# Attention with an MLP behind it: q's scale factor moves into GpSimd's cast, k and q are cast ahead of v, and four loads move behind a DMA transpose

## Chip, cores, metric

One core of a Trainium2 chip runs the whole program. The metric is the device time of one execution in microseconds. Engines are named as the profile names them: PE (TensorE), PEld (its weight loads), DVE (VectorE), ACT (ScalarE), POOL (GpSimd), SP (SyncE, which here only issues DMAs).

## The reference

Attention over 8 batches of 12 heads with 448 positions of 64 numbers, with a softmax that has one more term in its denominator, then an MLP with a Mish-like gate over the 3584 tokens. q, k, v, the weights and the output are f32.

```python
def _attn_ref(q, k, v):                      # each (8, 12, 448, 64)
    scale = 1.0 / np.sqrt(q.shape[-1])       # 1/8
    scores = scale * np.matmul(q, k.transpose(0, 1, 3, 2))
    m = np.max(scores, axis=-1, keepdims=True)
    e = np.exp(scores - m)
    attn = e / (np.sum(e, axis=-1, keepdims=True) + np.exp(-m) + 1e-09)
    return np.matmul(attn, v)

def _moe_ref(x, w_in, w_out):                # x (3584, 768), w_in (768, 2048), w_out (2048, 768)
    h = x @ w_in
    sp = np.where(h > 20.0, h, np.log1p(np.exp(np.minimum(h, 20.0))))
    return (h * np.tanh(sp)) @ w_out
```

## The kernel before

**Pairs and units.** Two heads of a batch are a pair; there are 48 pairs, 6 to a batch. Three pairs are a unit (`UNIT_PAIRS`), so a batch is two units and pair p belongs to unit p // 3. The first six pairs run in a loop of their own (the head). The main loop then runs over units `u`, with `p0 = 3u` the unit's first pair and `nxt = p0 + 3` the next unit's first pair. A unit has 12 steps `n` (four a pair) of attention, mixed with pieces of the second MLP product (L567), and then eight blocks `f` of the first MLP product (L514) of a batch whose attention is done. Attention ends with unit 15; what follows is MLP alone.

**A pair's way.** SP loads q, k and v of a pair (`load_pair`, L135), each as 112 rows of 512 f32 numbers, into buffers of which there are three for each of q, k and v. `cast` turns them to bf16 on POOL (L186); from pair 1 on all casts are POOL's. q and k must then be turned so that the head's 64 numbers lie along the partitions. Up to pair 17 PE does this and DVE copies the result out with the factor 1/8. From pair 18 on (`BY_DMA_FROM`), `turn_by_dma` (L197) has two DMA transposes do it, one for the three k of a unit and one for its three q; then `evac_qk` writes each pair's q into the block-diagonal tile `qd` (two halves of 64 partitions, one for each head), with the factor 1/8, as two POOL instructions (L268). The scores (L327) are PE's; DVE takes the negative maximum (L348), ACT the exponentials (L361) into `en`. At the end of a unit's steps DVE divides (`normalise`, L430), and a DMA transpose on SP turns `en` into `eT` (L438). In the next unit PE multiplies `eT` by v (`av_pair`, L478): the products of pairs p0-3, p0-2 and p0-1 stand in PE's order just ahead of the fourth score step of pairs p0, p0+1 and p0+2, and the scores run three steps ahead of the exponentials, so they come at about n = 0, 4 and 8.

**When things are issued.** Each engine and SP's queue work in the order written here. In units 2 to 4 loads and casts are spread over steps 0, 3 and 6. From unit 5 on, step 0 does it all for a unit: POOL copies two numbers out of the unit before's last `en` into `marks` (L714), which holds POOL back until that is divided; then the casts and the transposes; then some loads:

```python
for p_ in range(p0 - UNIT_PAIRS + 1, p0 + 1):      # the v casts
    if "v" in loaded.get(p_, ()):
        cast(p_, "v")
for i in range(UNIT_PAIRS):                        # the k and q casts of the next unit
    cast(nxt + i, "kq")
turn_by_dma(nxt)
load_pair(nxt + UNIT_PAIRS, "kq")
for i in range(UNIT_PAIRS):
    load_pair(p0 + 1 + i, "v")
```

So v is loaded for pairs p0+1 to p0+3 and cast in the next unit: unit 6 (p0 = 18) casts v of 16, 17, 18. In unit 5 only v of pair 15 is left to cast. In units 5 to 14 there are k and q to cast; unit 15 casts v only.

The k and q of the two remaining pairs of the unit after next are loaded at step 11 (`n == steps - 1`), from unit 4 on (`u >= first_mm2`, where `first_mm2` is 4). In unit 4 these are pairs 19 and 20. The first blocks of the first MLP product follow: at f = 0 the unit's first pair is divided and its transpose issued (pair 12 in unit 4), at f = 3 and f = 7 the other two (13 and 14), which are divided there.

Weights of the second MLP product are still being loaded through POOL's queue (L169) during unit 4.

Of the kernel before, what the change touches and what calls it, by code (L numbers as in the profile page):

```python
# [12 lines left out]
ALU = mybir.AluOpType  # L13
AX = mybir.AxisListType

UNIT_PAIRS = 3
# [3 lines left out]
def kernel(  # L20
# [9 lines left out]
    nc = tc.nc  # L30

    B, H, S, D = q.shape
# [14 lines left out]
    SCALE = 1.0 / float(D) ** 0.5  # L47
# [55 lines left out]
    QB = S // 64  # L103
# [68 lines left out]
    def cast(p, names):  # L172
        if p >= N_PAIRS:
            return
        by_t = "p h (t d) -> p t h d"
        to = casted.setdefault(p, {})
        for nm in names:
            src = loaded[p].pop(nm)
            if nm != "v":
                to[nm] = (q_cast if nm == "q" else k_cast)[:, p % UNIT_PAIRS]  # L180
            else:
                to[nm] = bf_pool.tile([SP_, 2, NT * D], BF16, tag="v_bf", name="v_bf", bufs=7)
            if nm != "v":
                src = src.rearrange(by_t, t=NT)
            if p > 0 or nm == "v":
                nc.gpsimd.tensor_copy(out=to[nm], in_=src)  # L186
                continue
            cuts = (0, NT) if nm == "k" else (0, NT // 2, NT)
            for lo, hi in zip(cuts, cuts[1:]):
                nc.vector.tensor_copy(out=to[nm][:, lo:hi], in_=src[:, lo:hi])  # L190
# [42 lines left out]
    def evac_qk(p, act=False):  # L233
        if p >= N_PAIRS:
            return
        by_dma = p >= BY_DMA_FROM
        by = nc.gpsimd if by_dma else nc.vector
        kT = kT_all[:, p % (2 * UNIT_PAIRS)]
        (q_ps, k_ps), own = ((qT_all[:, p % UNIT_PAIRS], kT), []) if by_dma else qkT[p]
        mo_free.extend(own)  # L240
        q_reads = []
        qd = q_diag[p % len(q_diag)]
        if p < DIAG_FROM:
            qT = qd.rearrange("d i h r -> d (i h r)")[:, 0:S]
            qkT[p] = (qT, kT)
            if p == 0:
                nc.scalar.copy(kT, k_ps[:, 0:S])
                by_2 = sc_tiles[2][:, 0, :].bitcast(BF16)
                for ps, half in (q_ps, slice(0, S // 2)), (by_2, slice(S // 2, S)):
                    nc.vector.tensor_scalar(  # L250
                        out=qT[:, half], in0=ps[:, half], scalar1=SCALE, scalar2=None,
                        op0=ALU.mult,
                    )
                return
            if act:
                nc.scalar.mul(qT, q_ps[:, 0:S], SCALE)
            else:
                q_reads.append(nc.vector.tensor_scalar(
                    out=qT, in0=q_ps[:, 0:S], scalar1=SCALE, scalar2=None, op0=ALU.mult
                ))  # L260
        else:
            qkT[p] = (qd, kT)
            if p < DIAG_FROM + len(q_diag):
                nc.vector.memset(qd[0:64, :, 1, :], 0.0)
                nc.vector.memset(qd[64:128, :, 0, :], 0.0)
            for h in range(2):
                rows = slice(64 * h, 64 * h + 64)
                q_reads.append(by.tensor_scalar(  # L268
                    out=qd[rows, :, h, :],
                    in0=q_ps[rows, 0:S].rearrange("d (i r) -> d i r", i=QB),  # L270
                    scalar1=SCALE, scalar2=None, op0=ALU.mult,
                ))
        if by_dma:
            return
        if own and not act:
            nc.vector.tensor_copy(out=kT, in_=k_ps[:, 0:S])
        else:
            k_read = nc.scalar.copy(kT, k_ps[:, 0:S])
            if not own:
                apart(k_read, *q_reads)  # L280
# [298 lines left out]
    steps = UNIT_PAIRS * STEPS  # L579
# [90 lines left out]
    for u in range(UNITS_PER_B, N_UNITS + 2 * UNITS_PER_B):  # L670
# [11 lines left out]
        for n in range(steps):  # L682
            pi, s = divmod(n, STEPS)
            p, idx = p0 + pi, p0 * STEPS + n
            late_tp = u == UNITS_PER_B and n == STEPS
            exps(idx)
            if u == UNITS_PER_B + 1 and n == 0:
                for j in range(2):
                    turn_on_pe(HEAD, j, busy_first=3)
            flush_late()  # L690
            if late_tp:
                transpose_pair(p0 + 2)
                evac_qk(p0 + 2)
            if held and n == 1:
                late.extend(held)
                held.clear()
                flush_late()
            late.extend(slow)
            slow.clear()
            acc += weight[n]  # L700
            want = int(total * acc / sum(weight) + 1e-6)
            while done < want:
                fn, w = filler.popleft()
                fn()
                done += w
            scores_ahead(end)
            if n in LOAD_AT and u <= first_mm2:
                at = p0 + LOAD_AT.index(n)
                load_pair(at + LEAD, "qk")
                load_pair(at + 1, "v")  # L710
                cast(at + LEAD - 1, "qk")
                cast(at, "v")
            elif n == 0 and u <= N_UNITS:
                nc.gpsimd.tensor_copy(  # L714
                    out=marks[0:1, 3, 0:2], in_=att[p0 - 1]["en"][0:1, NT - 1, NTILE - 1, 0:2]
                )
                for p_ in range(p0 - UNIT_PAIRS + 1, p0 + 1):
                    if "v" in loaded.get(p_, ()):
                        cast(p_, "v")
                for i in range(UNIT_PAIRS):  # L720
                    cast(nxt + i, "kq")
                turn_by_dma(nxt)
                load_pair(nxt + UNIT_PAIRS, "kq")
                for i in range(UNIT_PAIRS):
                    load_pair(p0 + 1 + i, "v")
            if s == 0 and u > first_mm2:
                evac_qk(nxt + pi)
            if n == steps - 1 and u >= first_mm2:
                for i in range(1, UNIT_PAIRS):
                    load_pair(nxt + UNIT_PAIRS + i, "kq")  # L730
            for pe, n0 in BY_PE.items():
                j = n - n0
                first = 2 if pe == HEAD else 0
                if pe // UNIT_PAIRS == u - 1 < first_mm2 - 1 and first <= j < NT:
                    turn_on_pe(pe, j, busy_first=1)
            spread = RDEN_AT.get(u - UNITS_PER_B, {})
            if n in spread:
                on_act = u < first_mm2
                spread_rden(
                    spread[n], copy=nc.scalar.copy if on_act else nc.vector.tensor_copy,  # L740
                    behind=slow if on_act else late,
                )
            early = AV_AT.get(u - UNITS_PER_B)
            if early is not None and n == 7:
                keep_busy(6, bank=mo_free[0])
            if early is not None:
                if n in early:
                    av_pair(early[n], half=p)
            elif s == (2 if pi else 0) and N_PAIRS <= p < N_PAIRS + UNIT_PAIRS:
                av_pair(p - UNIT_PAIRS)  # L750
            if u - UNITS_PER_B < len(W_AT):
                at = (u - UNITS_PER_B, n)
                load_w(W_AT[at[0]].get(n, 0), behind=W_BEHIND.get(at))
# [5 lines left out]
        for f in range(FF_U):  # L759
            if moe:  # L760
                mm1_mish(b, w * FF_U + f)
            if u == UNITS_PER_B and f == 3:
                load_w(3, behind=p0 + 2)
            if not attn:
                continue
            if f == 0:
                denominators(p0, UNIT_PAIRS)
                for p in todo if p0 < LATE_DIV else todo[:1]:
                    normalise(p, dma=p not in BY_PE)
            if f == 5 and u == UNITS_PER_B + 1:  # L770
                spread_rden(p0, copy=nc.scalar.copy)
            if f == 4:
                scores_ahead(min(nxt * STEPS + 1, N_PAIRS * STEPS))
            if f in (1, 3, 5):
                if nxt < BY_DMA_FROM:
                    transpose_pair(nxt + f // 2, bank=f // 2 % 2)
                    evac_qk(nxt + f // 2)
            if f >= FF_U - 2:
                scores_ahead(min(nxt * STEPS + f - FF_U + 4, N_PAIRS * STEPS))
            if f in (3, FF_U - 1) and p0 >= LATE_DIV:  # L780
                p = todo[1 + f // (FF_U - 1)]
                normalise(p, dma=p not in BY_PE)
# [32 lines left out]
```

## Time and profile before

| | us |
|---|---|
| median of 3 runs | 471.48 (470.95 to 472.93) |
| the profiled execution, its own time | 475.91 |
| its span, first to last instruction | 474.1 |
| mean granted clock of TensorE in it | 0.993 |

| engine | busy us | instructions |
|---|---|---|
| PE | 449.2 | 3051 |
| DVE | 347.5 | 657 |
| ACT | 331.6 | 877 |
| POOL | 180.8 | 258 |

How to read the rows that follow. A group's row has line, engine, operation, what it writes and reads, partitions x elements with types, how often; then busy us, mean ns of one, idle us of the engine just before them and what ended that. A timeline's row has start (us from the span's start), length in us, engine, line and operation; rows of like instructions on end are merged (x3), and a bracket gives the idle time ahead of it. "SPq" is SP's queue: an issued DMA, whose length is the time of issuing it. A row of a stage's busy times has the window, its length, then busy us (and count) of PE, PEld, DVE, ACT and POOL, the granted clock, the DMA engines' share and GB/s.

### The profile page before, as it was taken

The numbers are of one execution on the slowest core, as the hardware profiler recorded it, in microseconds if no ns is written. First come the engines' busy times: TensorE is split into PE (matmuls) and PEld (weight loads), VectorE is DVE, ScalarE is ACT, GpSimd is POOL, SyncE is SP. The second block draws the span as 40 slices with busy tenths as digits, with TensorE's granted clock in tenths as the row PEclk, the third lists the DMA queues.
The fourth block names the chain that finished last, engine by engine and source line by source line (L and its number), as shares of the span: only waits on it lengthen the run. The fifth ranks groups of instructions, "written<-read, shape, count | busy, mean of one in ns | idle before, by whom it ended". The sixth has DMA issues, their size and how long they took to land.

```text
span 474.1 us, 8841 instructions
## 1 busy us (share of the span) xinstructions
PE 449.2 (95%) x3051; PEld 245.8 (52%) x3051; DVE 347.5 (73%) x657; ACT 331.6 (70%) x877; POOL 180.8 (38%) x258
## 2 busy tenths in 40 slices
PE   7778888999889999999999999999999999999996
PEld 3344445555535555555555555555555555556563
DVE  5999738759859798989898888989798979421021
ACT  5998848879747887978686869687887869211300
POOL 4613609105126455455463644646464620100000
PEclk9999999999989999999999999999999999999999
DMA  8999999999999999999999999999999594921122
GB/s 253 228 115 244 220 216 209 174 214 252 185 239 280 222 273 231 261 250 230 259 233 287 212 224 242 282 233 268 217 273 235 155 213 128 225 76 33 35 57 77
DMA packets 232493, 97.94 MB, mean 207 GB/s; under 512 B 189312, under 2 KB 228992, under 8 KB 232448
## 3 DMA queue, kind: packets, MB, share of 16 engines
q1 hardware_dynamic: 224928, 91.06, 84.9%
q0 software_dynamic: 7488, 6.29, 9.2%
q8 instruction: 24, 0.39, 0.4%
q14 instruction: 21, 0.17, 0.1%
q10 hardware_dynamic: 32, 0.02, 0.0%
HBM read 45.61 MB, written 11.01 MB: 119 GB/s over the span
## 4 chain that ended last, share of the span: by engine, by line
PE 68%; ACT 6%; DVE 5%; DMA 3%; issue 1%; SPq 0%; DVEq 0%; ACTq 0%
PE mo L514 24%; PE mo L567 24%; PE sc L327 8%; PE sc L478 6%; ACT en L361 6%; DVE negm L348 4%; PE sc L514 4%; DMA eT<-en 3%; PE mo L478 1%; DVE xT L491 1%; PE mo L288 0%; DMA out_dram<-o_sb 0%; DVE o_sb L550 0%; PE sc L220 0%; DVE eT L453 0%
## 5 line engine op out<-in xcount | busy, mean ns | idle before, releaser
L361 ACT ACTIVATE en<-sc,negm 128x448 bf16<-128x448 f32 x336 | 208.8, 643 | 27.3 <-DVE negm L348 25.5
L348 DVE TENSOR_REDUCE negm<-sc 128x2 f32<-128x896 f32 x192 | 182.6, 970 | 50.2 <-PE sc L327 39.6
L567 PE MATMUL mo<-w_out_sb,gT 128*128 128x384 bf16 (+1 forms) x1024 | 167.4, 307 | 0.4 <-DVE rb L418 0.4
L514 PE MATMUL mo<-xT,w_in_sb 128*128 128x448 bf16 x672 | 139.0, 352 | 2.8 <-DMA w_in_sb<-in_moe_w_in_dram 2.6
L567 PEld LDWEIGHTS <-gT 128*128 128x128 bf16 x1024 | 96.6, 98 | 56.6 <-issue 2.9
L520 ACT ACTIVATE gT<-mo 128x448 bf16<-128x448 f32 x112 | 59.4, 543 | 82.2 <-PE mo L514 81.8
L514 PEld LDWEIGHTS <-w_in_sb 128*128 128x128 bf16 x768 | 74.0, 98 | 72.0 <-DMA w_in_sb<-in_moe_w_in_dram 3.8
L268 POOL TENSOR_SCALAR qd<-qT_all 64x448 bf16<-64x448 bf16 x60 | 80.1, 1335 | 61.7 <-DMA qT_all<-q_cast 32.6
L430 DVE TENSOR_SCALAR en<-en,rden 128x448 bf16<-128x448 bf16 x252 | 85.5, 413 | 0.5
L361 ACT ACTIVATION_READ_ACCUMULATOR en<-sc,negm 128x1 f32 x336 | 72.2, 215 | 0.0
L327 PE MATMUL sc<-kT_all,qd 128*128 128x448 bf16 x252 | 72.2, 356 | 0.0
L550 DVE COPY o_sb<-mo 128x384 f32<-128x384 f32 (+1 forms) x64 | 31.9, 498 | 48.3 <-PE mo L567 48.1
L478 PE MATMUL sc<-eT,v_bf 112*64 112x448 bf16 x336 | 40.2, 360 | 5.4 <-DMA eT<-en 3.6
L186 POOL CAST q_cast<-q_f 112x512 bf16<-112x512 f32 x47 | 28.6, 608 | 32.6 <-PE mo L409 18.6
L327 PEld LDWEIGHTS <-qd 128*128 128x128 bf16 x252 | 24.7, 98 | 29.2 <-issue 13.4
L714 POOL COPY marks<-en 1x2 bf16<-1x2 bf16 x12 | 2.1, 175 | 96.3 <-DVE en L430 96.3
L478 PEld LDWEIGHTS <-v_bf 112*64 112x64 bf16 x384 | 20.0, 109 | 24.1 <-issue 7.4
L186 POOL CAST k_cast<-k_f 112x512 bf16<-112x512 f32 x47 | 28.5, 607 | 0.6 <-DMA k_f<-in_k_dram 0.3
L186 POOL CAST v_bf<-v_f 112x512 bf16<-112x512 f32 x48 | 28.1, 605 | 1.5 <-DMA v_f<-in_v_dram 1.1
L514 PE MATMUL sc<-xT,w_in_sb 128*128 128x448 bf16 x96 | 20.8, 352 | 0.0
L491 DVE CAST xT<-sc 128x448 bf16<-128x448 f32 x33 | 20.3, 615 | 0.0
L520 ACT ACT_TABLE_LOAD x14 | 18.0, 1283 | 0.8 <-PE mo L514 0.3
(63 smaller groups left out, 245.2 us busy)
## 6 DMA issues: line engine op xcount, KB each, us to landing
k_f<-in_k_dram SPq DMA_DIRECT2D x48, 224.0 KB, 5.0
q_f<-in_q_dram SPq DMA_DIRECT2D x48, 224.0 KB, 4.8
v_f<-in_v_dram SPq DMA_DIRECT2D x48, 224.0 KB, 5.1
w_in_sb<-in_moe_w_in_dram POOLq DMA_DIRECT2D x12, 256.0 KB, 10.7
w_out_sb<-in_moe_w_out_dram POOLq DMA_DIRECT2D x8, 384.0 KB, 13.3
out_dram<-o_sb SPq DMA_DIRECT2D x7, 336.0 KB, 4.1
out_dram<-o_sb SPq DMA_DIRECT2D x8, 288.0 KB, 5.1
out_dram<-o_sb SPq DMA_DIRECT2D x8, 240.0 KB, 3.7
```

Source lines behind the costliest of these rows:

```text
L186: nc.gpsimd.tensor_copy(out=to[nm], in_=src)
L268: q_reads.append(by.tensor_scalar(out=qd[rows, :, h, :], in0=q_ps[rows, 0:S].rearrange("d (i r) -> d i r", i=QB), scalar1=SCALE, scalar2=N ...
L327: nc.tensor.matmul(sc[:, bk, 0:S], lhsT=qT[:, i].rearrange("d h r -> d (h r)"), rhs=kT, start=True, stop=True,)
L348: half_max[p] = nc.vector.tensor_reduce(out=negm, in_=sc[:, 0 : len(cols), 0:S], axis=AX.X, op=ALU.max, negate=True)
L361: e = nc.scalar.activation(out=st["en"][:, :, c, 0:SP_], in_=sc[:, bk, 0:S].rearrange("q (j c) -> q j c", j=NT), func=AF.Exp, bias=st["neg ...
L430: nc.vector.tensor_scalar(out=en[:, :, i, 0:SP_], in0=en[:, :, i, 0:SP_], scalar1=st["rden"][:, i : i + 1], scalar2=None, op0=ALU.mult,)
L478: mm = nc.tensor.matmul(av[h * 64 : (h + 1) * 64, 0:S], lhsT=v_bf[:, h, j * D : (j + 1) * D], rhs=e_h, start=(j == 0), stop=(j == NT - 1),)
L491: read = nc.vector.tensor_copy(out=to, in_=av[:, 0:S])
L514: nc.tensor.matmul(h_ps[:, 0:S], lhsT=w_in_sb[:, dm, ff * 128 : (ff + 1) * 128], rhs=xT[b][:, dm, :], start=(dm == 0), stop=(dm == DM_T - 1),)
L520: nc.scalar.activation(out=gT[:, ff, b % 2 * S : b % 2 * S + S], in_=h_ps[:, 0:S], func=AF.Mish)
L550: nc.vector.tensor_copy(out=o_sb[:, cols.start : cols.start + n_dve], in_=st["o"][:, 0:n_dve])
L567: nc.tensor.matmul(st["o"][:, 0:n_cols], lhsT=gT[:, ff, i * 128 : (i + 1) * 128], rhs=w_out_sb[:, ff, cols], start=(ff == 0), stop=(ff == ...
```

## The change

Three edits, and the factor 1/8 is applied once in either version:

- For pairs from 18 on, q's cast on POOL (112x512, f32 to bf16) becomes a multiplication by 1/8 of the same tile (30 instructions in units 5 to 14). The 60 POOL multiplications that wrote `qd` become plain copies of the same 64x448 bf16 numbers.
- At step 0 of units from 5 on, the k and q casts stand ahead of the v casts in POOL's order. In SP's order nothing moves by this.
- In unit 4, the loads of q and k of pairs 19 and 20 are issued after the transpose of pair 12 instead of at step 11 ahead of it. On SP they now stand between the transposes of pairs 12 and 13. Later units keep their place.

```diff
@@ cast
+            if nm == "q" and p >= BY_DMA_FROM:
+                nc.gpsimd.tensor_scalar(
+                    out=to[nm], in0=src, scalar1=SCALE, scalar2=None, op0=ALU.mult
+                )
+                continue
             if p > 0 or nm == "v":
                 nc.gpsimd.tensor_copy(out=to[nm], in_=src)
                 continue
@@ evac_qk
-        by = nc.gpsimd if by_dma else nc.vector
...
-                q_reads.append(by.tensor_scalar(
-                    out=qd[rows, :, h, :],
-                    in0=q_ps[rows, 0:S].rearrange("d (i r) -> d i r", i=QB),
-                    scalar1=SCALE, scalar2=None, op0=ALU.mult,
+                q_h = q_ps[rows, 0:S].rearrange("d (i r) -> d i r", i=QB)
+                if by_dma:
+                    nc.gpsimd.tensor_copy(out=qd[rows, :, h, :], in_=q_h)
+                    continue
+                q_reads.append(nc.vector.tensor_scalar(
+                    out=qd[rows, :, h, :], in0=q_h, scalar1=SCALE, scalar2=None, op0=ALU.mult,
                 ))
@@ the main loop, step 0
+                for i in range(UNIT_PAIRS):
+                    cast(nxt + i, "kq")
                 for p_ in range(p0 - UNIT_PAIRS + 1, p0 + 1):
                     if "v" in loaded.get(p_, ()):
                         cast(p_, "v")
-                for i in range(UNIT_PAIRS):
-                    cast(nxt + i, "kq")
                 turn_by_dma(nxt)
@@ the main loop, step 11
-            if n == steps - 1 and u >= first_mm2:
+            if n == steps - 1 and u > first_mm2:
                 for i in range(1, UNIT_PAIRS):
                     load_pair(nxt + UNIT_PAIRS + i, "kq")
@@ the main loop, first MLP product, f == 0
                 for p in todo if p0 < LATE_DIV else todo[:1]:
                     normalise(p, dma=p not in BY_PE)
+                if u == first_mm2:
+                    for i in range(1, UNIT_PAIRS):
+                        load_pair(nxt + UNIT_PAIRS + i, "kq")
```

## The prediction

> **What bounds the kernel now.** I read the page first: engines, the chain of waits, the costliest groups.
>
> ```profile
> span 474.1 us, 8841 instructions
> ...
> PE 449.2 (95%) x3051; PEld 245.8 (52%) x3051; DVE 347.5 (73%) x657; ACT 331.6 (70%) x877; POOL 180.8 (38%) x258
> ...
> PE 68%; ACT 6%; DVE 5%; DMA 3%; issue 1%; SPq 0%; DVEq 0%; ACTq 0%
> ...
> L268 POOL TENSOR_SCALAR qd<-qT_all 64x448 bf16<-64x448 bf16 x60 | 80.1, 1335 | 61.7 <-DMA qT_all<-q_cast 32.6 <-PE sc L327 13.5 <-PE sc L478 12.0
> ```
>
> PE sets the end; POOL, which most of the change touches, is busy for 38%. An average over stages hides what matters, so I cut the steady part into units (a unit is three pairs, some 25.3 us) and asked for each stage's busy times:
>
> ```profile
> 159.60:185.30 25.70, 25.27 (x168) 14.45 (x169) 22.88 (x43) 20.22 (x55) 13.24 (x17) 1.00 1.13 244
> 185.30:210.60 25.30, 25.30 (x152) 13.20 (x153) 22.63 (x42) 20.20 (x54) 13.12 (x17) 1.00 1.06 261
> ...
> 337.20:362.50 25.30, 25.30 (x152) 13.20 (x153) 21.91 (x42) 20.25 (x54) 13.12 (x17) 1.00 0.99 247
> ```
>
> The first numbers are the window, its length and PE's busy time: 25.27 of 25.70, then 25.30 of 25.30. PE has no slack in a steady unit. Making POOL cheaper there brings nothing, and any wait that PE is given is paid in full. The one DMA wait of the chain lies earlier. In order of time the chain shows it, and PE's timeline shows the gap:
>
> ```profile
> 118.32 14.29 DMA eT<-en
> ```
>
> ```profile
> 132.66 1.38 PE L478 MATMUL sc<-eT,v_bf 112*64 112x448 bf16 x8 [3.58 <-DMA eT<-en]
> 139.19 0.95 PE L478 MATMUL sc<-eT,v_bf 112*64 112x448 bf16 x8
> 144.12 0.95 PE L478 MATMUL sc<-eT,v_bf 112*64 112x448 bf16 x8
> ```
>
> PE stands still for 3.58 us, from 129.08, until the turning of pair 12 lands at 132.6. These three rows are the value products (L478) of pairs 12, 13 and 14.
>
> **Part one: the four loads.** SP's timeline before that wait:
>
> ```profile
> 111.45 0.31 SPq L135 DMA_DIRECT2D k_f<-in_k_dram  x1
> 111.82 0.45 SPq L135 DMA_DIRECT2D q_f<-in_q_dram  x1
> 114.65 0.31 SPq L135 DMA_DIRECT2D k_f<-in_k_dram  x1
> 115.02 0.45 SPq L135 DMA_DIRECT2D q_f<-in_q_dram  x1
> 118.32 19.90 SPq L438 DMA_TRANSPOSE eT<-en  x3
> ```
>
> The first four rows are the loads of pairs 19 and 20, issued before the three turnings of unit 4. The transfers run without a gap, and their rate stands last here:
>
> ```profile
> 111.45:118.30 6.85, 6.85 (x55) 4.17 (x55) 6.07 (x16) 6.51 (x18) 5.14 (x8) 1.00 1.11 270
> ```
>
> Four loads of 224 KB are 0.92 MB, and 0.92 MB at 270 GB/s is 3.4 us of transfers that no longer lie ahead of pair 12's turning. It lands at about 132.66 - 3.4 = 129.3, against 129.08 when PE wants it: 0.2 us of wait is left. The wait had a second price, read from the granted clock (the last number but two):
>
> ```profile
> 129.62:133.03 3.41, 0.38 (x4) 0.25 (x6) 0.00 (x0) 1.49 (x6) 3.20 (x6) 1.00 1.25 233
> 133.04:136.44 3.40, 3.40 (x14) 1.32 (x11) 1.16 (x2) 0.72 (x2) 0.00 (x0) 0.50 1.30 219
> ```
>
> PE was busy for 0.38 of 3.41 us, and the next 3.40 us ran at half the clock. From pair 12's product to pair 13's are 6.53 us here (139.19 - 132.66), from pair 13's to pair 14's 4.93: the half clock cost 1.6. Stall and clock together are 3.58 + 1.6 = 5.2 us.
>
> Not all of that is won, because the loads now stand ahead of pair 13's turning, the next thing in SP's queue:
>
> ```profile
> L438 SPq DMA_TRANSPOSE eT<-en x1: 3738/3738/3738, 130.5 to 130.5; - x1
> ...
> DMA to landing us min/median/max: 6.8/6.8/6.8
> ```
>
> It was issued at 130.5 and landed 6.8 later, at 137.3. Now its issue follows pair 12's 3.4 us earlier but four load issues later (0.8 us a pair by the rows above, so 1.6): at 128.7, landing at 135.5 if the loads ahead of it cost nothing, at 138.9 if they cost all their 3.4. I take the middle, 137.2. PE wants it at 139.19 - 5.2 + 0.2 = 134.2, so 3.0 us of wait come back. Part one gains 5.2 - 0.2 - 3.0 = 2.0 us, bounds 0 (all comes back) and 5.2. In POOL's queue the casts of pairs 19 and 20 now wait for these loads, and v's cast behind them. The cover is wide: pair 18's diagonal copies run from 143.57, its first score (the x2 row) follows at 151.69, and both are shifted alike.
>
> ```profile
> 143.57 6.96 POOL L268 TENSOR_SCALAR qd<-qT_all 64x448 bf16<-64x448 bf16 x5 [10.76 <-DMA qT_all<-q_cast]
> ```
>
> ```profile
> 151.69 0.54 PE L327 MATMUL sc<-kT_all,qd 128*128 128x448 bf16 x2
> ```
>
> **Part two: the order and price of the casts.** Each unit from 6 on starts with a mark on POOL, three v casts, then six casts of k and q. Of the v casts the first one is wanted soonest: v is loaded one unit ahead for pairs p0+1 to p0+3, so unit 6 casts v of 16, 17, 18, and its PE stream multiplies by v of 15, 16, 17. Hence the second value product of a unit (pair 16) waits for the first v cast of that same unit. POOL, then PE:
>
> ```profile
> 159.31 0.17 POOL L714 COPY marks<-en 1x2 bf16<-1x2 bf16 x1 [7.37 <-DVE en L430]
> 159.43 1.72 POOL L186 CAST v_bf<-v_f 112x512 bf16<-112x512 f32 x3
> 161.10 0.60 POOL L186 CAST k_cast<-k_f 112x512 bf16<-112x512 f32 x1
> 161.66 0.60 POOL L186 CAST q_cast<-q_f 112x512 bf16<-112x512 f32 x1
> ...
> 163.89 0.60 POOL L186 CAST q_cast<-q_f 112x512 bf16<-112x512 f32 x1
> ```
>
> ```profile
> 159.57 0.95 PE L478 MATMUL sc<-eT,v_bf 112*64 112x448 bf16 x8
> ...
> 164.50 0.95 PE L478 MATMUL sc<-eT,v_bf 112*64 112x448 bf16 x8
> ```
>
> Before, that cast was done 0.72 us after the mark, and PE came for it 164.50 - 159.31 = 5.19 us after. In the last unit that the change touches the distance is the same, 5.20:
>
> ```profile
> 362.20 0.17 POOL L714 COPY marks<-en 1x2 bf16<-1x2 bf16 x1 [7.27 <-DVE en L430]
> ```
>
> ```profile
> 367.40 0.95 PE L478 MATMUL sc<-eT,v_bf 112*64 112x448 bf16 x8
> ```
>
> From 159.31 to 362.20 are eight periods, so nine units, 6 to 14 (unit 5 casts only v of 15, wanted in unit 6; unit 15 casts no k or q).
>
> Now the first v cast comes behind three k casts and three q operations that are no longer casts but multiplications. A cast's pitch is 0.56 us (161.10 to 161.66). What a GpSimd multiplication of 112x512 f32 costs no row shows, so it is bounded from both sides:
>
> ```profile
> L268 POOL TENSOR_SCALAR qd<-qT_all x60: 1321/1334/1522, 143.6 to 378.7; 64x448 bf16<-64x448 bf16 x60
> ```
>
> ```profile
> L714 POOL COPY marks<-en 1x2 bf16<-1x2 bf16 x12 | 2.1, 175 | 96.3 <-DVE en L430 96.3
> ```
>
> Below stands the cast of the same tile, 0.60 us. Above stands the multiplication of 448 elements, 1335 ns, scaled to 512: 1.53, or with a fixed 0.175 (the two-element copy) 0.175 + 1.16 x 512/448 = 1.50. It is the same operation on the same engine, only its source is f32 and its shape differs; per element it takes 2.98 ns where the cast takes 1.18. I take 1.50. Then the first v cast ends 0.12 + 3 x 0.56 + 3 x 1.50 + 0.60 = 6.9 us after the mark, where PE comes at 5.2: a wait of 1.7 us. Behind it in PE's queue stand the pair's last score and the out-projection, and DVE's maximum and ACT's exponentials wait for that score. As PE has no slack and the next mark follows PE through DVE's L430, each unit pays anew: 9 x 1.7 = 15.3 us. PE first waits when a q operation costs more than (5.2 - 0.12 - 1.68 - 0.60) / 3 = 0.93 us.
>
> The Trainium skill speaks against this price: "GPSIMD Engine Reference", section 4.1, calls one-input elementwise work on GpSimd roughly line-rate. By that q's factor would cost what its cast does, and the sum would hold only part one's gain; this trace has 2.98 ns an element against it for a one-input multiplication.
>
> The rest is hidden. The plain diagonal copies should cost near the cast's 0.53 us for 448 instead of 1335 ns (bounds 0.5 and 1.34): no matter, since nothing waits for L268 beyond the 8 us cover shown for pair 18. The turnings of k and q wait for casts that end at 6.3 after the mark instead of 5.2, when SP is still issuing k's turning. The v loads on SP wait for v casts that end 8.0 after the mark, and SP came to them later than that:
>
> ```profile
> 165.37 1.35 SPq L197 DMA_TRANSPOSE kT_all<-k_cast  x1
> ...
> 169.62 1.46 SPq L135 DMA_DIRECT2D v_f<-in_v_dram  x3
> ```
>
> These are 6.1 (for 1.35 us) and 10.3 after the mark of 159.31.
>
> **The sum.** 15.3 - 2.0 = 13.3 us more. The profiled execution took 475.91 us, 1.8 of it outside its span of 474.1, and comes to 489.2. The median of the runs shown is 471.48, 4.4 below the profiled one, and gives 484.8.
>
> **The rivals.**
>
> *The multiplication is cheap* (not slower). If an f32 source makes it run like the cast, at 0.60, the first v cast ends 4.1 us after the mark, PE never waits, and part one alone counts: 471.5 - 2.0 = 469.5, between 466.3 and 471.5. For it speaks that the cast's f32 input runs at 1.18 ns an element; against it, that 60 multiplications lie tightly at 1.33 us. It decides as long as a q operation stays under 0.93 us.
>
> *A price between*, 0.93 to 1.33 us: waits of 0 to 1.2 us in nine units, so about 470 to 480, middle 475.
>
> *Each new wait also halves the clock.* It did after the 3.58 us. A window with 1.7 us of wait is half busy; one with 0.38 of 3.41 lost its clock. This would add up to 1.6 us to each of nine units: 484.8 + 14.4 = 499. Against it: before that, at
>
> ```profile
> 61.40:64.80 3.40, 1.97 (x16) 0.90 (x14) 0.39 (x1) 1.17 (x3) 0.00 (x0) 1.00 1.35 158
> ```
>
> 1.97 of 3.40 us busy kept the whole clock. The Trainium skill ("TensorE: Matmul & The Clock Gate", part 1) lets the clock fall after an idle window of about 3.4 us; by that a wait of 1.7 does not halve it.
>
> *Part one does nothing*: the weights' transfers, not the four loads, hold pair 12 back. Then 2.0 us more, 486.8; it lies in the forecast's range.
>
> **How the numbers follow.** The dear multiplication 0.70, the cheap one 0.18, the price between 0.07, the clock 0.05. Own range of the likeliest: a price of 1.33 and the whole 5.2 gained, 9 x 1.2 - 5.2 = +5.6, 477; a price of 1.60 (1.53 and the 0.07 us that lie between two L268), 9 x 2.0 and nothing gained, +18, 489.5. The range goes down to 469 to take in the middle case and half of the cheap one. About 0.5%, 2.4 us, can be told from no change. The cheap case is about at that edge: 0.12 faster, 0.06 same. The middle gives 0.01, 0.01 and 0.05 slower. Together 0.13, 0.07, 0.80.
>
> **What would show it.** Right: q's group on POOL at about 1.5 us; PE's second value product in units 6 to 14 waiting some 1.7 us for a v cast; a unit of 27.0 us instead of 25.3; pair 12's wait almost gone, one of pair 13's in its place. Wrong: q's group under 0.93 us, units still of 25.3; half a clock in steady units; or pair 12's wait unchanged.

## The result, and the profile after

| | us |
|---|---|
| after, median of 6 runs | 489.84 (483.57 to 492.96) |
| before, median of 6 runs | 471.22 (469.15 to 472.93) |
| ratio, with its 95% interval | 1.0338 (1.0261 to 1.0416) |
| predicted | 484.8 (469 to 489.5) |

Slower, as forecast. The ratio leaves out runs over 1.5% above the fastest of their kernel, here two of the six after (the profiled one among them), so it is smaller than the ratio of the medians. Times the 471.48 us shown at first it gives 487.4; the median of the six runs lies 0.3 us above the end of the range. The profiled execution took 491.58 us with a span of 489.5, against 475.91 and 474.1 before. The spread of the runs after, 9 us, has a cause of its own (below).

From the page of the profile after, the engines, the chain of waits and three groups. The first number behind the bar is the busy time, then the mean ns of one, then the idle time ahead:

```profile
span 489.5 us, 8860 instructions
...
PE 451.1 (92%) x3051; PEld 246.0 (50%) x3051; DVE 327.3 (67%) x657; ACT 332.6 (68%) x877; POOL 161.3 (33%) x258
...
PE 30%; issue 22%; POOL 17%; DMA 11%; DVE 3%; ACT 2%; POOLq 0%; SPq 0%; DVEq 0%
...
L484 PE MATMUL sc<-eT,v_bf 112*64 112x448 bf16 x336 | 40.6, 363 | 20.7 <-POOL v_bf L191 14.0
...
L186 POOL TENSOR_SCALAR q_cast<-q_f 112x512 bf16<-112x512 f32 x30 | 44.4, 1478 | 0.0
L274 POOL COPY qd<-qT_all 64x448 bf16<-64x448 bf16 x60 | 33.3, 556 | 31.0 <-DMA qT_all<-q_cast 28.4
```

POOL is busy for 19.5 us less than before, and yet it now stands in the chain of waits with 17%, where it had no share at all. q's multiplication takes 1478 ns, the plain diagonal copy 556. The value products (L478 before, L484 now) wait for POOL's v cast for 14.0 us in all. One unit in the two timelines of after, POOL and PE:

```profile
160.32 0.17 POOL L720 COPY marks<-en 1x2 bf16<-1x2 bf16 x1 [12.10 <-DVE en L436]
160.45 0.60 POOL L191 CAST k_cast<-k_f 112x512 bf16<-112x512 f32 x1
161.02 1.48 POOL L186 TENSOR_SCALAR q_cast<-q_f 112x512 bf16<-112x512 f32 x1
...
165.04 1.48 POOL L186 TENSOR_SCALAR q_cast<-q_f 112x512 bf16<-112x512 f32 x1
166.48 1.71 POOL L191 CAST v_bf<-v_f 112x512 bf16<-112x512 f32 x3
```

```profile
167.13 0.95 PE L484 MATMUL sc<-eT,v_bf 112*64 112x448 bf16 x8 [1.56 <-POOL v_bf L191]
...
382.80 0.95 PE L484 MATMUL sc<-eT,v_bf 112*64 112x448 bf16 x8 [1.56 <-POOL v_bf L191]
```

The first v cast starts at 166.48 and is done at 167.07, 6.75 us after the mark; PE starts at 167.13, after 1.56 us of standing still. The last row is the same wait in unit 14. In between there is one in each unit, nine in all. The stages of after show what they do to a unit's length (window, length, PE's busy time first):

```profile
187.86:214.75 26.89, 25.35 (x151) 13.14 (x150) 20.18 (x42) 20.30 (x54) 11.18 (x17) 1.00 0.99 235
...
349.37:376.26 26.89, 25.35 (x150) 13.15 (x150) 20.18 (x42) 20.36 (x54) 11.18 (x17) 1.00 0.92 236
```

A unit takes 26.89 us where it took 25.30, and PE works for the same 25.3 of it. The granted clock stays at 1.00, so these waits do not cost clock.

In unit 5 the wait has moved from pair 12 to pair 13. PE's timeline of after, SP's, and the busy times around the second wait:

```profile
128.94 0.95 PE L484 MATMUL sc<-eT,v_bf 112*64 112x448 bf16 x8 [0.15 <-DMA eT<-en]
...
138.71 1.71 PE L484 MATMUL sc<-eT,v_bf 112*64 112x448 bf16 x8 [4.79 <-DMA eT<-en]
```

```profile
126.96 0.53 SPq L135 DMA_DIRECT2D k_f<-in_k_dram  x1
...
128.54 0.46 SPq L135 DMA_DIRECT2D q_f<-in_q_dram  x1
129.10 10.55 SPq L444 DMA_TRANSPOSE eT<-en  x2
```

```profile
135.03:138.44 3.41, 0.00 (x0) 0.00 (x0) 0.00 (x0) 1.48 (x6) 0.47 (x1) 1.00 1.26 257
138.52:141.92 3.40, 3.21 (x13) 1.37 (x14) 0.91 (x2) 0.25 (x1) 0.00 (x0) 0.50 1.22 278
```

Pair 12's 3.58 us have become 0.15, pair 13's none have become 4.79, and the half clock (0.50, the last number but two) has moved along.

Cut at POOL's marks, which every unit from 5 on starts with, the two executions differ like this (the last columns are mark 5 to mark 6, mark 6 to mark 15, and mark 15 to the end of the span):

| execution | start to mark 5 | unit 5 | units 6 to 14 | rest | span |
|---|---|---|---|---|---|
| before | 128.78 | 30.52 | 228.21 | 86.59 | 474.1 |
| after | 128.50 | 31.83 | 242.60 | 86.59 | 489.5 |

Of the 15.4 us, 14.4 lie in the nine units and 1.3 in unit 5; the rest of the span is the same to 0.01 us.

### The profile page after: what moved, and what is told of

Read it like the earlier page. It is cut to its first block, busy times and chain, and to the rows that moved or that the text cites. A ratio compares the mean times of both kernels' runs of the same rounds, so it can differ in the third digit from the quotient of the medians.

```text
span 489.5 us, 8860 instructions
## 1 busy us (share of the span) xinstructions
PE 451.1 (92%) x3051; PEld 246.0 (50%) x3051; DVE 327.3 (67%) x657; ACT 332.6 (68%) x877; POOL 161.3 (33%) x258
## 4 chain that ended last, share of the span: by engine, by line
PE 30%; issue 22%; POOL 17%; DMA 11%; DVE 3%; ACT 2%; POOLq 0%; SPq 0%; DVEq 0%
PE mo L573 11%; PE mo L520 10%; POOL q_cast L186 8%; DMA eT<-en 5%; DMA qT_all<-q_cast 5%; POOL qd L274 5%; POOL k_cast L191 3%; PE sc L484 3%; PE sc L333 2%; PE sc L520 2%; DVE negm L354 1%; ACT en L367 1%; POOL v_bf L191 1%; PE mo L484 1%; PE mo L294 0%
## 5 line engine op out<-in xcount | busy, mean ns | idle before, releaser
L367 ACT ACTIVATION_READ_ACCUMULATOR en<-sc,negm 128x1 f32 x336 | 71.2, 212 | 0.0
L436 DVE TENSOR_SCALAR en<-en,rden 128x448 bf16<-128x448 bf16 x252 | 64.3, 332 | 0.5
L484 PE MATMUL sc<-eT,v_bf 112*64 112x448 bf16 x336 | 40.6, 363 | 20.7 <-POOL v_bf L191 14.0
L186 POOL TENSOR_SCALAR q_cast<-q_f 112x512 bf16<-112x512 f32 x30 | 44.4, 1478 | 0.0
L274 POOL COPY qd<-qT_all 64x448 bf16<-64x448 bf16 x60 | 33.3, 556 | 31.0 <-DMA qT_all<-q_cast 28.4
L484 PEld LDWEIGHTS <-v_bf 112*64 112x64 bf16 x384 | 19.5, 110 | 40.7 <-POOL v_bf L191 17.4
L191 POOL CAST q_cast<-q_f 112x512 bf16<-112x512 f32 x17 | 10.5, 620 | 31.1 <-DMA q_f<-in_q_dram 30.9
## 6 DMA issues: line engine op xcount, KB each, us to landing
w_out_sb<-in_moe_w_out_dram POOLq DMA_DIRECT2D x8, 384.0 KB, 11.1
```

What stands on the lines that cost most here:

```text
L186: nc.gpsimd.tensor_scalar(out=to[nm], in0=src, scalar1=SCALE, scalar2=None, op0=ALU.mult)
L274: nc.gpsimd.tensor_copy(out=qd[rows, :, h, :], in_=q_h)
L367: e = nc.scalar.activation(out=st["en"][:, :, c, 0:SP_], in_=sc[:, bk, 0:S].rearrange("q (j c) -> q j c", j=NT), func=AF.Exp, bias=st["neg ...
L436: nc.vector.tensor_scalar(out=en[:, :, i, 0:SP_], in0=en[:, :, i, 0:SP_], scalar1=st["rden"][:, i : i + 1], scalar2=None, op0=ALU.mult,)
L484: mm = nc.tensor.matmul(av[h * 64 : (h + 1) * 64, 0:S], lhsT=v_bf[:, h, j * D : (j + 1) * D], rhs=e_h, start=(j == 0), stop=(j == NT - 1),)
```

## The experiments

Each timed kernel was compared with runs of the kernel before on the same chip; the medians of those runs were 470.5 to 472.5 us, and they spread from 467.5 to 477.4.

**The loads back at their old place**, all else as changed.

```diff
-            if n == steps - 1 and u > first_mm2:
+            if n == steps - 1 and u >= first_mm2:
...
-                if u == first_mm2:
-                    for i in range(1, UNIT_PAIRS):
-                        load_pair(nxt + UNIT_PAIRS + i, "kq")
```

> The changed kernel with the four loads back at their old place. Theory (nine waits of PE for the first v cast, 1.6 us each, are the whole loss): the nine waits stay at 1.5 to 1.6 us, units 6 to 14 stay at 26.9 us, and pair 12's wait of about 3.6 us returns in place of pair 13's of 4.8; about 471.2 + 14.4 = 485.6 us, 1 to 2 under the changed kernel's profiled execution. Rival (the loads carry a good part of the loss and the spread of its runs): 475 to 480, runs close together.

Measured: 483.04 us (482.32 to 488.28), ratio 1.0269 (1.0206 to 1.0331). The nine waits stand (13.1 us in all; unit 6's is the only short one, 0.72), units 6 to 14 take 242.60 us, and pair 12 waits 3.32 us again. The loss survives without the loads' move, so the rival falls. Whether the move adds to it can't be read from the two ratios, whose intervals overlap.

**The loads' move alone**, on the kernel before (the same lines the other way round).

> The kernel before with only the four loads moved behind pair 12's turning. Theory: pair 12's wait goes, pair 13's of 4 to 5 us comes, with half the clock after it; no other wait; 471 to 473.5 us. Rival (as predicted, part one gains): 469 or less, because pair 13's wait is made by the multiplications on GpSimd and not by the loads ahead of its turning.

Measured: 472.94 us (467.44 to 478.60), ratio 0.9987 (0.9940 to 1.0033): no difference that can be told. In the profiled execution pair 12 does not wait and pair 13 waits 2.18 us, half of the 4 to 5 expected, followed by half the clock. So pair 13's wait comes with the loads and needs no multiplication on GpSimd; the gain that the prediction gave this part does not show.

**The order alone**, on the kernel before: k and q are cast ahead of v, q by a plain cast.

```diff
+                for i in range(UNIT_PAIRS):
+                    cast(nxt + i, "kq")
                 for p_ in range(p0 - UNIT_PAIRS + 1, p0 + 1):
                     if "v" in loaded.get(p_, ()):
                         cast(p_, "v")
-                for i in range(UNIT_PAIRS):
-                    cast(nxt + i, "kq")
```

> The kernel before with only the casts of k and q ahead of v's; q's cast stays a cast of 0.60 us. Theory: the first v cast ends 0.12 + 6 x 0.56 + 0.60 = 4.1 us after the mark, PE comes at 5.2 and does not wait; 471 us, units of 25.3. Rival (the order by itself costs, through v's loads or the turnings): units longer than 25.5 and more than 473 us.

Measured: 473.83 us (467.89 to 475.51), ratio 0.9997 (0.9944 to 1.0051), units 6 to 14 in 228.21 us. POOL and PE in unit 6 of this kernel:

```profile
151.77 0.17 POOL L714 COPY marks<-en 1x2 bf16<-1x2 bf16 x1 [7.43 <-DVE en L430]
...
155.24 1.72 POOL L186 CAST v_bf<-v_f 112x512 bf16<-112x512 f32 x3
```

```profile
156.97 0.95 PE L478 MATMUL sc<-eT,v_bf 112*64 112x448 bf16 x8
```

The first v cast ends 4.1 us after the mark, PE comes at 5.2 and has no bracket: no wait. The order costs nothing while the casts ahead are cheap.

**The factor alone**, on the kernel before: q is multiplied in the cast and `qd` copied, but v is cast first.

```diff
+            if nm == "q" and p >= BY_DMA_FROM:
+                nc.gpsimd.tensor_scalar(
+                    out=to[nm], in0=src, scalar1=SCALE, scalar2=None, op0=ALU.mult
+                )
+                continue
... (and the plain diagonal copies, as in the change)
```

> The kernel before with only q's factor moved into GpSimd's cast and plain diagonal copies; v is cast first. Theory: no wait for a v cast, the last k and q casts end 1.68 + 0.12 + 1.68 + 4.4 = 7.9 us after the mark and the turnings start 2 us later without anybody waiting; 471 us, units of 25.3. Rival (the dear multiplication costs by itself, because the turnings of k and q or the diagonal copies come too late): PE waits for L274 or the turnings, over 473 us.

Measured: 471.06 us (467.63 to 475.76), ratio 0.9980 (0.9940 to 1.0021). The 30 multiplications cost 1478 ns here too, and nobody waits for a v cast; the nine units take 229.43 us, 1.2 more than before: two first products wait for a transpose of `en`, 0.22 us at 157 us and 0.80 at 234. Over the runs the price alone costs nothing that can be told either: the loss needs both edits at once.

**Two dear ones of three.** As the kernel with the loads back, but the middle pair of a unit keeps a plain cast and its factor in the diagonal copy.

```diff
-            if nm == "q" and p >= BY_DMA_FROM:
+            if nm == "q" and p >= BY_DMA_FROM and p % UNIT_PAIRS != 1:
... (and the middle pair's diagonal copy multiplies again)
```

> The kernel with the loads back, but of a unit's three q only two are multiplied in the cast; the middle pair keeps a plain cast and its factor in the diagonal copy. Theory (PE waits for the end of a sum on GpSimd): the first v cast ends 1.5 - 0.57 = 0.9 us sooner after the mark, so PE's wait in units 6 to 14 is 1.55 - 0.9 = 0.6 us, units of 26.0 us, about 471.5 + 9 x 0.65 = 477.5 us. Rival (PE waits once a unit whatever the amount, for instance because a wait of any length costs a fixed restart): waits near 1.5 us and 483 us as with three.

Measured: 479.73 us (476.10 to 481.50), ratio 1.0164 (1.0100 to 1.0228). The waits of PE in this kernel:

```profile
PE sc L489 <- POOL v_bf L191: 5.9, 9, 0.7
```

Nine waits again, 5.9 us in all, 0.66 each where three multiplications gave 1.55. One multiplication less took 0.9 us off each, as the sum on POOL says, and the units fell from 26.95 to 26.06 us (234.56 / 9). The whole time lies 2 us above the expectation: unit 5 took 29.46 us in the profiled execution. As only four runs were taken, it is the nine waits that speak here, more than the median.

**One v cast first**, then k and q, then the other two v casts; the factor in the cast, the loads at their old place.

```diff
+                for p_ in range(p0 - UNIT_PAIRS + 1, p0 - UNIT_PAIRS + 2):
+                    if "v" in loaded.get(p_, ()):
+                        cast(p_, "v")
                 for i in range(UNIT_PAIRS):
                     cast(nxt + i, "kq")
```

> The kernel with the loads back and the dear multiplication, but the one v cast that the unit itself needs (pair p0-2) stands ahead of k and q, the other two behind them. Theory: no wait for the first v cast; the second v cast (pair p0-1) ends 0.12 + 0.56 + 1.68 + 4.45 + 0.60 = 7.4 us after the mark, where PE comes at 10.1, so it doesn't wait either; 471.5 us, units of 25.3. Rival (the v casts behind the multiplications hurt as a whole): waits remain at the third product, over 474 us.

Measured: 469.57 us (467.39 to 474.78), ratio 0.9991 (0.9951 to 1.0030), units 6 to 14 in 228.21 us. POOL and PE in unit 6 of this kernel:

```profile
152.95 0.60 POOL L191 CAST v_bf<-v_f 112x512 bf16<-112x512 f32 x1
...
159.52 1.16 POOL L191 CAST v_bf<-v_f 112x512 bf16<-112x512 f32 x2
```

```profile
158.02 0.95 PE L484 MATMUL sc<-eT,v_bf 112*64 112x448 bf16 x8
...
163.27 0.95 PE L484 MATMUL sc<-eT,v_bf 112*64 112x448 bf16 x8 [0.42 <-ACT en L367]
```

Moving one instruction of 0.60 us takes back the whole loss. The second v cast ends at 160.1, the product that needs it starts at 163.27 and waits for ACT, as it did before.

**The loads one transpose further**, behind pair 13's turning, first on the kernel before, then with one v cast first and the factor in the cast.

```diff
-            if n == steps - 1 and u >= first_mm2:
+            if n == steps - 1 and u > first_mm2:
...
                 p = todo[1 + f // (FF_U - 1)]
                 normalise(p, dma=p not in BY_PE)
+                if u == first_mm2 and f == 3:
+                    for i in range(1, UNIT_PAIRS):
+                        load_pair(nxt + UNIT_PAIRS + i, "kq")
```

> The kernel before with the four loads moved one transpose further, behind pair 13's turning instead of behind pair 12's. Theory (whatever stands right behind the four loads in SP's queue is late): pair 12's and pair 13's turnings land before PE comes, at most pair 14's is late by 1 to 2 us, and no window is idle enough to halve the clock; 468 to 470.5 us. Rival (the weights' transfers and not the loads hold the turnings back): a wait of 2 us or more stays at pair 12 or 13, 471 us or more.

> One v cast first, the factor in the cast, and the four loads behind pair 13's turning. Theory: no wait for a v cast and none of over 2 us at pairs 12 to 14, so as the kernel with the loads behind pair 13, 468 to 470.5 us. Rival (the later and longer casts of pairs 19 and 20 delay the turnings of k and q of unit 6): a wait at the scores of pair 18, over 471 us.

Measured: 469.46 us (467.89 to 478.59), ratio 0.9996 (0.9959 to 1.0033), and 471.08 us (468.26 to 474.79), ratio 1.0018 (0.9980 to 1.0056). Neither profiled execution has a wait at pairs 12 to 14, nor the second one at the scores of pair 18 (unit 5 takes 25.25 us in both), and yet neither kernel is faster than the one before over its runs. A kernel whose profile shows no wait at pair 12 runs like one whose profile shows 3.58 us: that wait can't be a fixed property of the kernel. The kernels with the order alone and with one v cast first pointed the same way. Their loads stand at the old place, and pair 12 did not wait in their profiles either. What did differ was older: the transpose of pair 8, issued at some 58 us, landed after 5.0 to 6.9 us in these four and after 13.6 in the first profile.

**Both kernels profiled once more**, unchanged.

> The kernel before, unchanged, profiled once more. Theory (pair 12's wait isn't a property of the kernel but of how an earlier turning, issued at some 58 us, met the weights' transfers in that execution): where that turning lands in 5 to 7 us, pair 12's wait is 0 and the time 467 to 470; where it takes 11 us or more, the wait is 1.8 to 3.6 and the time 472 to 476. Rival (the wait belongs to the loads ahead of pair 12's turning, and the executions differ for another reason): 3.6 us of wait again whatever that turning took.

> The changed kernel, unchanged, profiled once more. Theory: the nine waits of 1.55 us stand again, and the rest follows the turning at 58 us: about 482 to 485 with little or no wait at pairs 12 and 13 where it lands in 5 to 7 us, 488 to 492 with a wait at pair 13 where it takes 11 or more. Rival: the wait at pair 13 is near 4.8 us in any case.

Measured: 468.38 us and 487.19 us, one run each. The kernel before shows no wait at pair 12 this time, and pair 8's transpose landed early. Its row, which is to be held against a landing after 13.6 us in the first execution:

```profile
L438 SPq DMA_TRANSPOSE eT<-en x1: 3534/3534/3534, 58.1 to 58.1; - x1
...
DMA to landing us min/median/max: 5.1/5.1/5.1
```

The changed kernel has its nine waits again (units 6 to 14 in 242.62 us) and a wait of 2.04 us at pair 13, after a landing in 11.1; its time lies 0.8 us under the 488 expected for that case. The profiled executions up to here side by side, in us:

| kernel | loads of 19 and 20 | pair 8 lands after | wait at 12 | wait at 13 | unit 5 |
|---|---|---|---|---|---|
| before | ahead of 12 | 13.6 | 3.58 | 0 | 30.52 |
| loads back | ahead of 12 | 12.2 | 3.32 | 0 | 28.64 |
| two dear | ahead of 12 | 12.5 | 2.53 | 0 | 29.46 |
| factor alone | ahead of 12 | 12.3 | 1.84 | 0.05 | 27.26 |
| before, again | ahead of 12 | 5.1 | 0 | 0 | 25.25 |
| order alone | ahead of 12 | 5.2 | 0 | 0 | 25.25 |
| one v first | ahead of 12 | 5.1 | 0 | 0 | 25.25 |
| after | behind 12 | 12.5 | 0.15 | 4.79 | 31.83 |
| loads alone | behind 12 | 11.5 | 0 | 2.18 | 29.09 |
| after, again | behind 12 | 11.1 | 0 | 2.04 | 28.95 |
| loads behind 13 | behind 13 | 6.9 | 0 | 0 | 25.25 |
| one v, loads behind 13 | behind 13 | 5.0 | 0 | 0 | 25.25 |

Where pair 8's transpose lands in 5 to 7 us there is no wait in unit 5, in any of the three places of the loads (the split below adds the missing case, behind 12). Where it takes 11 or more, somebody waits: pair 12 with the loads ahead of it, pair 13 with the loads ahead of that one. An execution with the loads behind pair 13 and a late pair 8 was not profiled.

What meets pair 8's transpose can be read from the bytes moved between 58 and 63 us: the queue of the weights moved 0.62 MB in the first execution of the kernel before and 0.02 in the second (0.46 in the execution that landed in 6.9 us, the slowest of the early ones). The executions part earlier still. Pair 1's transpose, issued at 19 to 21 us, landed after 9.7 to 11.5 us in the five without a wait in unit 5 and after 15.3 to 17.9 in the seven others; the weights that can meet pair 8's were issued from 46.4 to 47.5 us in the five and from 48.8 to 51.9 in the seven.

**The weights split.** If a transpose is slow because weights are in flight, less of them at a time should help from the start of the program.

```diff
-            if s == 3 and p == 1:
-                load_w(2)
+            if s == 0 and p in (1, 2):
+                load_w(1)
```

> The kernel before with the first two transfers of w_in no longer issued together behind pair 1's last step but one each at the first steps of pairs 1 and 2, so that fewer bytes of weights are in flight when a turning starts. Theory (a turning that meets the weights' transfers takes two to three times as long, and the loss is handed on from there): the turnings of pairs 1 and 2 land sooner, the one at 58 us in 5 to 7 us in most executions, median 468 to 470 us and no run over 473. Rival (the variation has another source): the runs lie between 467 and 476 as before.

Measured: 468.10 us (467.39 to 469.46, 12 runs), ratio 0.9951 (0.9923 to 0.9978). The runs of the kernel before beside it lay between 467.60 and 474.62. In the profiled execution pair 8's transpose lands in 5.1 us and unit 5 takes 25.25. It is the one version here that is faster than both kernels, by about half a percent: its fastest run is no faster than theirs (467.39 against 467.60), but none is late. Pair 1's transpose landed in 10.8 us, against 16.2 and 10.9 in the two profiles of before, so it is again the early kind; what makes pair 1's land early or late in the unsplit kernel is not settled.

**The changed kernel with the weights split.**

> The changed kernel with w_in's first two transfers split as in the kernel that ran at 468.1 us. Theory (two separate losses): the turning at 58 us lands in 5 to 7 us in nearly every execution, so the spread goes, and the nine waits alone remain on top of 468.1: 468.1 + 9 x 1.6 = 482.5 us, runs within 3 us of one another; at pairs 12 and 13 a wait of under 1 us, since the weights are through before the loads start. Rival (the loads behind pair 12's turning cost a wait at pair 13 in any state): a wait of 2 us or more at pair 13, half the clock after it, and 485 us or more.

Measured: 483.02 us (482.58 to 484.26), ratio 1.0265 (1.0208 to 1.0323). Pair 8's transpose lands in 5.0 us, pair 12 does not wait and pair 13 waits 0.07, unit 5 takes 25.37 and the nine units 242.73. The rival falls: with pair 8 early the loads behind pair 12 cost next to nothing. Against the 468.10 of the same split on the kernel before (measured on another chip), the order and the price together cost 14.9 us, and the runs of each kernel lie within 2.1 us of one another.

## Why the prediction was right, and where it was off

- *PE has no slack in a steady unit, so a wait is paid in full.* Right. PE's busy time in a unit stayed at 25.3 us, each wait of 1.54 to 1.56 us made its unit 1.60 us longer, and what lies behind the last of them is unchanged.
- *The price of q's multiplication, 1.50 us, between 0.60 and 1.53.* Right: 1478 ns, 2.89 an element where the bf16 one took 2.98. An f32 source makes it hardly cheaper. The rival with the cheap multiplication fell by this alone, and so did the price between. The line-rate rule of "GPSIMD Engine Reference", section 4.1 of the Trainium skill, holds in these runs for casts and copies (1.19 ns an element for k's cast, 1.24 for the diagonal copy) and not for the multiplication.
- *The first v cast ends 6.9 us after the mark, PE comes at 5.2.* 6.75 and 5.2. The nine waits, 15.3 forecast, sum to 14.0, and the nine units grew by 14.4. The difference is mostly the pitch of a multiplication: from 161.02 to 166.48 lie three of them and two casts of 0.56, so 1.45 each where 1.50 was taken, 0.15 us a unit.
- *Threshold and dose.* The order with cheap casts gave no wait, two multiplications 0.66, three 1.55: the wait is the sum on POOL less 5.2, as written.
- *What was called hidden was hidden.* The diagonal copies went from 1335 to 556 ns and the rest of POOL's day moved, and no unit was shorter or longer for it.
- *Each wait halves the clock* did not come: the nine units ran at 1.00.
- *Part one gains 2.0 us.* This step failed. Its first half was right for the execution it was read from: pair 12 was to land at 129.3 with 0.2 us of wait left, and landed at 128.9 with 0.15. The second half was mis-sized: pair 13's turning was to be issued at 128.7, to land at 137.2 and leave 3.0 us of wait; it was issued at 129.1, landed 9.5 later at 138.6, and left 4.79. And the sum counted the half clock as won for good; it came back behind pair 13. Unit 5 took 1.3 us more instead of 2.0 less. In three other executions with the loads at that place pair 13 waited 2.18, 2.04 and 0.07 us, so the 4.79 is no constant either. Deeper lay the assumption that the 3.58 us belong to the kernel. They belong to executions in which an earlier transpose was late, so over many runs the move makes no difference that can be told (0.9987, 0.9940 to 1.0033).
- *The sum.* Forecast for the profiled execution were 489.2 us, and it took 491.58. Part one came out 3.3 us dearer and the nine units 0.9 cheaper, so the two errors partly cancel, which is luck. That the first two profiles both show a late transpose, and so can be compared, is luck as well. With part one at nothing the sum would have been 15.3 us; the two kernels with the split weights lie 14.9 apart.
- *Part one does nothing* was listed as a rival, for another reason (the weights hold pair 12 back). Its time, 486.8, is within 1 us of the ratio's 487.4, but what the runs show is not its mechanism as written: the move did relieve pair 12, and the wait came back one pair later.

## What to carry to other kernels

In an in-order queue of an engine that is idle two thirds of the time, look for the first item of what is pushed back and for who comes for it when; the price of a move is the length of what now stands ahead less that distance, once in every repetition, and one item put back can undo it. Cheaper work on an engine that bounds nothing gains nothing, while its order can cost. And before a wait in one profile is credited to an edit, profile the same kernel again: here a wait of 3.58 us, the longest that PE had, was absent from the next execution.

## What the runs showed of the hardware that was not expected

A DMA transpose that meets other transfers is slowed by more than their bytes would take. Pair 8's landed in 5.0 to 5.2 us where few or no weights moved beside it, and its issuing held SP for 3.5. In the first execution of the kernel before, the weights' queue moved 0.88 MB between 57.5 and 71 us, which at the 217 GB/s moved there is some 4 us (an estimate); the transpose took 8.5 us longer to land than in the second execution and held SP for 10. In the late executions the transposes of pairs 8 and 12 took 8 to 14 us to land and held SP for 6 to 12, so that whatever stood behind them on SP was late as well.

The half clock needs less than an empty window, and a wait of over 3 us need not bring it. In the kernel with the loads alone, then in the one with the loads back (PE's busy time is the number behind the length):

```profile
131.50:134.90 3.40, 1.22 (x11) 0.63 (x11) 1.72 (x2) 3.21 (x11) 0.00 (x0) 1.00 1.29 171
134.94:138.30 3.36, 3.36 (x14) 1.19 (x9) 1.16 (x2) 0.72 (x2) 0.00 (x0) 0.50 1.20 273
```

```profile
126.78:130.19 3.41, 1.90 (x12) 0.93 (x10) 1.82 (x8) 3.40 (x12) 1.79 (x3) 1.00 1.30 165
130.19:133.61 3.42, 1.62 (x13) 0.82 (x14) 0.27 (x1) 0.53 (x2) 3.42 (x5) 1.00 1.25 277
133.61:137.02 3.41, 3.41 (x22) 1.83 (x22) 3.41 (x6) 2.09 (x7) 1.61 (x2) 1.00 1.26 163
```

A wait of 2.18 us cost the next 3.4 us half their clock; one of 3.32 us cost none. The Trainium skill ("TensorE: Matmul & The Clock Gate", part 1) has windows of about 3.4 us that run freely, and by that it matters where in such a window a wait falls; these two executions agree. The traces show the grid: in each execution the changes of the granted clock lie whole multiples of 3.41 us apart (in the kernel with the loads alone at 25.69, 134.91 and 138.33 us). The rows above are cut on it. The wait of 2.18 us fell into one stretch, that of 3.32 us was shared by two. Between 100 us and the last matmuls, stretches with PE busy for 1.37 us or less were followed by half the clock (0.00, 0.38, 0.88, 1.22 and 1.37 in five executions), and those with 1.57 or more were not (1.57, 1.62; the nine waits leave 1.8 or more). Near 23 us, in the head, half the clock also followed stretches with 1.8 to 2.0 us busy, so the busy time alone does not decide; what else counts is open.

DVE's divisions got faster with POOL's shorter diagonal copies: L430 took 413 ns on average before, and L436 takes 332 after (353 with the factor alone, 408 with the order alone). Before, the 106 divisions that ran mostly beside a diagonal multiplication on POOL took 528 ns on average and the other 146 took 329; after, none runs mostly beside a diagonal copy. With the factor alone 26 did, and took 565. So it is the overlap that costs. Some 20 us of DVE's time were saved in this way, and none of the program's.
